# The second chunk of a first pass by seven products instead of eight, with the weights rounded in another order

## The chip, the cores and the metric

The kernel runs on one core of a Trainium2 chip. The metric is the device time of one execution in microseconds, the median of several runs. The engines of the core are TensorE (PE; its weight loads are listed as PEld), VectorE (DVE), ScalarE (ACT), GpSimd (POOL) and SyncE (SP), which issues the transfers.

## The reference

Two parts follow each other: a retention attention (8 batches, 8 heads, 576 tokens, 64 dimensions), and a two-layer block on its output with the activation h * erf(softplus(h)).

```python
scores = scale * np.matmul(q, k.transpose(0, 1, 3, 2))
Dmat = np.where(rel >= 0, gamma ** rel, 0.0)          # decay, gamma by head
attn_out = np.matmul(scores * Dmat, v)
x = attn_out.transpose(0, 2, 1, 3).reshape(B * S, H * D)   # 4608 x 512
h = x @ w_in                                          # w_in 512 x 2048
sp = np.maximum(h, 0.0) + np.log1p(np.exp(-np.abs(h)))
g = h * erf(sp)
return g @ w_out                                      # w_out 2048 x 512
```

## The kernel before

The 4608 tokens are nine chunks of 512, and d_ff is cut into four groups. The kernel walks all nine chunks for group 0, then for group 1, and so on (36 blocks). During group 0 it computes the attention as well, in stages that it deals out between the products: a stage is the transposes of q and k, the scores, or the outputs of 128 tokens.

A block has a first product set (x by w_in, `First`) and a second one (g by w_out, `Second`). Each is a 2 x 2 block product done by seven products of sums instead of eight (Winograd's form): four sums of the operands on each side, seven products of four matmuls each, accumulated in three PSUM tiles (a, e and g), some of which go on accumulating after they have been copied out. The first two chunks of group 0 are the exception: they use `plain`, the eight products, as 16 half-products of two matmuls.

The seven products of a block (`plain` and what is around it cut to what matters):

```python
PLAIN = 2

def operands_x(g, c):
    summed.add((g, c))
    t = x[g, c]
    # b11, b12, b21, b22: the quarters of x; t1, t2, t4: room for sums
    # ...
    if g == 0 or c < PLAIN:
        tt(t1, b12, b11, ALU.subtract)
        tt(t2, b22, t1, ALU.subtract)
        tt(b12, b22, b12, ALU.subtract)
    else:                                   # b12 was stored as the sum already
        tt(t2, b12, b11, ALU.add)
        tt(t1, b22, t2, ALU.subtract)
    if g == 0:
        store_x(c)                          # for the later groups
    tt(t4, b21, t2, ALU.subtract)
    x[g, c] = {A11: b11, A12: b21, S4: b22, A22: t4, S1: t1, S2: t2, S3: b12}

class First:
    def first(self):
        # ... a, e: PSUM tiles; t1: 128 x 2 x 512
        self.product(A11, self.a, True)
        nc.scalar.copy(out=self.t1[:, 0], in_=self.a)
        yield
        self.product(A12, e, True)
        tt(self.t1[:, 0], e, self.t1[:, 0], ALU.add)
        yield

    def middle(self):
        # ...
        self.product(S2, self.a, False)
        nc.scalar.copy(out=self.t1[:, 1], in_=self.a)
        yield
        self.product(S3, self.e, True)
        yield
        self.product(S1, self.a, False)
        nc.scalar.copy(out=self.t2[:, 1], in_=self.a)
        tt(self.t2[:, 1], self.e, self.t2[:, 1], ALU.add)
        yield

    def last(self):
        self.product(S4, self.a, False)
        nc.scalar.copy(out=self.t2[:, 0], in_=self.a)
        yield
        self.product(A22, self.e, False)
        tt(self.t1[:, 1], self.e, self.t1[:, 1], ALU.add)
        self.softplus()
        yield

    def plain(self):
        # four PSUM tiles; 4 x 4 half-products of two matmuls, a yield after each
        # after the last of a tile: nc.scalar.copy(out=(t2 if tok else t1)[:, f], in_=acc[n])

    def softplus(self):                     # ScalarE: 2 x 1024 columns
    def erf(self):                          # ScalarE: 2 x 1024 columns
    def multiply(self):                     # VectorE: t1 * s, t2 * s
    def sums(self):                         # VectorE: four sums of the activations
```

The weights come as raw parts and are rounded in steps; `round_weights(n)` issues n steps. Parts 1 to 4 of group 0 are w_in, parts 5 to 8 w_out. A part has five steps (ScalarE's two instructions first, then VectorE's, then GpSimd's multiplication and addition; for the first group's w_in VectorE does those too). After the last part of a matrix come four steps that are the four sums of its blocks:

```python
yield src, "wa", g, a, dc % 2, ["wa"] if g > 0 and dc == n_dc - 1 else []
# ...
sums = (["wb"] if g > 0 else ["wb", "wa"]) if (f, j) == (1, GP - 1) else []
yield src, "wb", g, B21 if f else B11, j, sums
```

The beginning is dealt out by a string (a: an attention stage, p: a half-product of the first chunk, w: the load of a part of the weights, a digit: so many steps of rounding, s: the store of x, k: matmuls that keep TensorE busy), then by a loop over the second chunk's half-products, then by the general loop:

```python
for what in "alkakakawkakakawwaa3awa2aaa5ppppaa5wwppa5ppawappwcppa5ppaaapp5s":
    # ...
most[0] = before_chunk(3)
attend(after_chunk(1))
store_x(1)
for step, _ in enumerate(firsts[1].plain()):
    if step % 2 == 0:
        attend(min(done[0] + 1, most[0]))
    round_weights(int(step > 1))
    if step == 1:
        firsts[0].softplus()
        firsts[0].erf()
    elif step == 5:
        firsts[0].multiply()
    elif step == 8:
        firsts[0].sums()
seconds[0].begin()
run(seconds[0].first(), (2, 2))       # two products, an attention stage after each
firsts[1].softplus()
most[0] = before_chunk(4)
for b, nxt in zip(blocks[2:], blocks[3:] + [None]):
    # ... the general loop: every later block by seven products
```

Of the kernel before, what the change touches and what calls it, by code (L numbers as in the profile page):

```python
# [2 lines left out]

# [1 line left out]

# [49 lines left out]
def kernel(  # L55
# [16 lines left out]
    n_dc = D_MODEL // P  # L72
    OH = D_MODEL // 2
    FH = D_FF // 2
    GP = 2
# [22 lines left out]
    def tt(out, in0, in1, op):  # L98
        nc.vector.tensor_tensor(out=out, in0=in0, in1=in1, op=op)  # L99
# [50 lines left out]
    def load(i, names="qkv"):  # L150
        if i < len(pieces):
            t = loaded.setdefault(i, {})
            for name in names:
                src = {"q": q, "k": k, "v": v}[name]
                if name == "q" and i < SQUARES:
                    t["q"] = load_rows(i, "q", q, 2)
                elif name == "q":
                    t["qs"] = load_squares(i, "q", q)
                    if i >= SQUARES_K:
                        t["ks"] = load_squares(i, "k", k)  # L160
                elif name == "v" or i < SQUARES_K or len(pieces[i]) == 1:
                    t[name] = load_rows(i, name, src, 4)
# [29 lines left out]
    def parts():  # L192

        w2 = w_in.rearrange("(e c d) (h f) -> c e d h f", c=n_dc, d=D, h=2)
        for g in range(n_g):
            for dc in range(n_dc):
                a = A11 if dc < 2 else A12
                src = [(heads[(e + dc) % 2], w2[dc, e, :, :, 2 * g * GW : 2 * (g + 1) * GW]) for e in range(2)]

                yield src, "wa", g, a, dc % 2, ["wa"] if g > 0 and dc == n_dc - 1 else []  # L200
            for f in range(2):
                for j in range(GP):
                    ft = f * FH // P + g * GP + j
                    src = [(slice(0, P), w_out[ft * P : (ft + 1) * P, :].rearrange("p (h o) -> p h o", h=2))]
                    sums = (["wb"] if g > 0 else ["wb", "wa"]) if (f, j) == (1, GP - 1) else []
                    yield src, "wb", g, B21 if f else B11, j, sums

    def sums_in(a11, s3, a12, a22, s1, s2, s4):
# [9 lines left out]
    def sums_out(b11, t3, b21, b22, t1, t2, t4):  # L218
# [7 lines left out]
        yield  # L226

    coming = parts()
    words = []
    most_g = [1]  # L230

    def load_weights():
        part = next(coming, None)
        if part is not None:
            t = wraw.tile([P, 2 * WP], UINT32, tag="wraw", name="wraw")
            for rows, src in part[0]:
                nc.sync.dma_start(out=t[rows].rearrange("p (h f) -> p h f", h=2), in_=src)
            words.append((t, *part[1:]))
# [49 lines left out]
    def round_weights(n=1):  # L288
        for _ in range(n):
            next(round_step, None)  # L290
# [149 lines left out]
    done = [0]  # L440

    def before_chunk(c):

        return stages.index((outputs, c * PC)) if c < n_ch else len(stages)

    def after_chunk(c):

        return stages.index((outputs, (c + 1) * PC - 1)) + 1

    def attend(upto):  # L450
        while done[0] < min(upto, len(stages)):
            of, i = stages[done[0]]
            of(i)
            done[0] += 1

    PLAIN = 2

    def load_x(g, c):  # L460
        x[g, c] = x_tile()
# [2 lines left out]
    def store_x(c):  # L464
        nc.sync.dma_start(out=xd[c], in_=x[0, c][:, :n_dc])
# [3 lines left out]
# [3 lines that stand above are left out]
        b11, b12, b21, b22 = (t[:, 2 * d : 2 * d + 2, h * TH : (h + 1) * TH] for d in range(2) for h in range(2))  # L472
        t1, t2, t4 = (t[:, n_dc + j, :].rearrange("p (d i) -> p d i", d=2) for j in range(3))
# [4 lines that stand above are left out]
        else:  # L478
# [3 lines that stand above are left out]
            store_x(c)  # L482
        tt(t4, b21, t2, ALU.subtract)
        x[g, c] = {A11: b11, A12: b21, S4: b22, A22: t4, S1: t1, S2: t2, S3: b12}
# [240 lines left out]
    firsts = [First(g, c) for g, c in order]  # L725
    seconds = [Second(f) for f in firsts]
# [8 lines left out]
    def keep_busy(n):  # L735
        for _ in range(n):
            nc.tensor.matmul(idle[:, :P], lhsT=ones, rhs=ones, start=True, stop=True)
# [4 lines left out]
    def run(steps, rounds=(), stages=1):  # L742

        for step, _ in enumerate(steps):
            attend(min(done[0] + stages, most[0]))
            round_weights(rounds[step] if step < len(rounds) else 0)
# [4 lines left out]

    for what in "alkakakawkakakawwaa3awa2aaa5ppppaa5wwppa5ppawappwcppa5ppaaapp5s":
        if what == "a":
            attend(done[0] + 1)
        elif what == "p":
            next(products)
        elif what == "s":
            store_x(0)  # L760
        elif what == "l":
            load(2, "kv")
        elif what == "c":
            nc.sync.dma_start(out=cst[:, CONST_FIRST:], in_=consts[:, CONST_FIRST:])
        elif what == "w":
            load_weights()
        elif what == "k":
            keep_busy(2)
        else:
            round_weights(int(what))  # L770
    most[0] = before_chunk(3)
    attend(after_chunk(1))
    store_x(1)
    for step, _ in enumerate(firsts[1].plain()):
        if step % 2 == 0:
            attend(min(done[0] + 1, most[0]))
        round_weights(int(step > 1))
        if step == 1:
            firsts[0].softplus()
            firsts[0].erf()  # L780
        elif step == 5:
            firsts[0].multiply()
        elif step == 8:
            firsts[0].sums()
    seconds[0].begin()
    run(seconds[0].first(), (2, 2))
    firsts[1].softplus()
    most[0] = before_chunk(4)
    for b, nxt in zip(blocks[2:], blocks[3:] + [None]):
        n = order.index((b.g, b.c))  # L790
# [9 lines left out]
        elif n + 2 < n_s:  # L800
            f = firsts[n + 1]
# [62 lines left out]
```

## Time and profile before

| what | value |
|---|---|
| time, median of 3 | 1027.61 us (1027.31 to 1028.06) |
| span of the profiled execution | 1024.0 us |
| transfers | 165.76 MB, mean 162 GB/s |
| instructions | 15958 |

In the profile, "L496" is line 496 of the kernel. L496 are the products of `First` by sums, L550 those of `plain`, L604 those of `Second`; L347 the scores, L365, L376 and L388 the outputs, L332 the transposes on TensorE and L326 those on VectorE. L99 is the helper `tt`, so its instructions are told apart by the tile that they write: x (with o as source: attention outputs; with x as source: sums), t, s, o, sT, wa, wb. L254 to L275 are the steps of rounding. One matmul of the source is two instructions in the profile (32-bit data), so a product of four matmuls is "x8".

The span in 40 equal slices of 25.6 us, as busy tenths, for orientation:

```profile
PE   9999999999999999999999999999999999999998
PEld 8787888888888888888888888888888888888887
DVE  3769777976976656656666666666567655555555
ACT  3354134234134444334343444444433333333332
POOL 2143112122312110010001001000100000000000
```

The change is in the second to fourth slice, where the attention, the rounding of the weights and the first chunks share the engines.

### The profile page before, as it was taken

What the parts mean: (1) busy time and instruction counts of PE and PEld (TensorE: products, weight loads), DVE (VectorE), ACT (ScalarE), POOL (GpSimd) and SP (SyncE); (2) the same over time, 40 slices, a digit from 0 to 9 for tenths busy, and PEclk for the clock granted to TensorE, in tenths of its full rate; (3) what the DMA queues carried; (4) which work ended last, traced back from release to release, by engine and by line L of the source; (5) the groups of instructions that cost most, each with busy time, mean ns of one, the idle gap of its engine ahead of it and who ended that gap; (6) DMA issues with size and microseconds to landing.
All of it is one profiled execution on the core that took longest, in us unless ns stands there. A gap on an engine that the chain in (4) does not pass through costs nothing.

```text
span 1024.0 us, 15958 instructions
## 1 busy us (share of the span) xinstructions
PE 1017.6 (99%) x6348; PEld 876.0 (86%) x6348; DVE 667.6 (65%) x1062; ACT 390.2 (38%) x481; POOL 122.6 (12%) x122
## 2 busy tenths in 40 slices
PE   9999999999999999999999999999999999999998
PEld 8787888888888888888888888888888888888887
DVE  3769777976976656656666666666567655555555
ACT  3354134234134444334343444444433333333332
POOL 2143112122312110010001001000100000000000
PEclk9999999999999999999999999999999999999999
DMA  9998989979974354544444345444433333444434
GB/s 200 203 242 175 232 203 223 255 150 253 244 195 150 106 161 145 165 160 154 164 147 158 124 147 162 165 144 144 144 124 124 124 131 127 131 136 131 126 88 119
DMA packets 146986, 165.76 MB, mean 162 GB/s; under 512 B 97376, under 2 KB 121568, under 8 KB 138848
## 3 DMA queue, kind: packets, MB, share of 16 engines
q1 hardware_dynamic: 144832, 163.57, 56.4%
q10 hardware_dynamic: 2080, 1.18, 0.5%
q8 instruction: 50, 0.82, 0.4%
q14 instruction: 24, 0.20, 0.1%
HBM read 117.52 MB, written 47.19 MB: 161 GB/s over the span
## 4 chain that ended last, share of the span: by engine, by line
PE 94%; DMA 3%; DVE 2%; SPq 1%; POOL 1%; issue 0%; ACTq 0%; DVEq 0%; POOLq 0%
PE a L604 24%; PE a L496 23%; PE g L604 12%; PE g L496 12%; PE e L496 6%; PE e L604 6%; PE o L365 3%; PE s L347 3%; PE o L388 2%; DMA raw_k<-in_k_dram 1%; PE o L376 1%; DMA raw_v<-in_v_dram 1%; PE f L668 1%; SPq L147 1%; PE p L550 1%; PE h L668 1%
## 5 line engine op out<-in xcount | busy, mean ns | idle before, releaser
L496 PE MATMUL a<-x,wa 128*128 128x256 f32 x1088 | 258.3, 380 | 0.0
L496 PEld LDWEIGHTS a<-x,wa 128*128 128x128 f32 x1088 | 205.7, 190 | 28.5
L604 PE MATMUL a<-wb,s 128*128 128x256 f32 x840 | 200.0, 381 | 0.0
L604 PEld LDWEIGHTS a<-wb,s 128*128 128x128 f32 x840 | 158.4, 190 | 22.9 <-ACT o L618 0.7
L99 DVE TENSOR_TENSOR t<-g,t 128x512 f32<-128x512 f32 x68 | 47.0, 691 | 151.9 <-ACT t L526 114.1
L496 PE MATMUL g<-x,wa 128*128 128x256 f32 x544 | 129.2, 380 | 0.0
L496 PEld LDWEIGHTS g<-x,wa 128*128 128x128 f32 x544 | 102.8, 190 | 14.4
L99 DVE TENSOR_TENSOR o<-a,o 128x512 f32<-128x512 f32 x104 | 71.4, 687 | 46.4 <-PE a L604 46.4
L521 ACT COPY t<-a 128x512 f32<-128x512 f32 x34 | 19.9, 586 | 188.3 <-PE a L496 188.3
L99 DVE TENSOR_TENSOR t<-t,s 128x1024 f32<-128x1024 f32 x72 | 88.4, 1267 | 0.0
L274 POOL TENSOR_TENSOR wraw<-wraw 128x512 f32<-128x512 f32 x28 | 29.4, 1051 | 438.1 <-DVE wraw L272 184.4
L565 ACT ACTIVATE s<-t 128x1024 f32<-128x1024 f32 x72 | 72.1, 1049 | 24.6 <-DVE t L99 24.5
L99 DVE TENSOR_TENSOR x<-x 128x512 f32<-128x512 f32 x115 | 75.8, 693 | 1.2
L532 ACT COPY t<-a 128x512 f32<-128x512 f32 x34 | 19.9, 586 | 144.4 <-PE a L496 144.4
L569 ACT ACTIVATE s<-s 128x1024 f32<-128x1024 f32 x72 | 72.1, 1049 | 0.4
L604 PE MATMUL g<-wb,s 128*128 128x256 f32 x280 | 66.7, 381 | 0.0
L604 PE MATMUL e<-wb,t 128*128 128x256 f32 x280 | 66.6, 380 | 0.0
L604 PE MATMUL a<-wb,t 128*128 128x256 f32 x280 | 66.6, 380 | 0.0
L604 PE MATMUL g<-wb,t 128*128 128x256 f32 x280 | 66.4, 380 | 0.0
L99 DVE TENSOR_TENSOR sT<-s,cst 128x512 f32<-128x512 f32 x72 | 46.2, 682 | 30.4 <-PE s L347 30.4
L496 PE MATMUL e<-x,wa 128*128 128x256 f32 x272 | 64.8, 381 | 0.0
L99 DVE TENSOR_TENSOR o<-g,o 128x512 f32<-128x512 f32 x70 | 47.9, 684 | 20.9 <-ACT o L618 18.1
(86 smaller groups left out, 1247.1 us busy)
## 6 DMA issues: line engine op xcount, KB each, us to landing
od<-o SPq DMA_DIRECT2D x54, 512.0 KB, 3.3
x<-xd SPq DMA_DIRECT2D x27, 1024.0 KB, 4.8
o<-od SPq DMA_DIRECT2D x27, 1024.0 KB, 5.4
raw_qs<-in_q_dram SPq DMA_DIRECT2D x96, 112.0 KB, 4.4
raw_ks<-in_k_dram SPq DMA_DIRECT2D x84, 112.0 KB, 4.2
xd<-x SPq DMA_DIRECT2D x9, 1024.0 KB, 5.2
raw_v<-in_v_dram SPq DMA_DIRECT2D x64, 128.0 KB, 4.5
wraw<-in_moe_w_in_dram SPq DMA_DIRECT2D x32, 256.0 KB, 5.7
```

Source lines behind the costliest of these rows:

```text
L99: nc.vector.tensor_tensor(out=out, in0=in0, in1=in1, op=op)
L274: engine.tensor_tensor(out=r_f, in0=high_f, in1=r_f, op=ALU.mult)
L347: nc.tensor.matmul(ps[e][:, p, :], lhsT=t["kT"][heads[e], p, :], rhs=t["qT"][heads[e], p, :], start=True, stop=True)
L365: nc.tensor.matmul(o[p % 2][heads[(e + p) % 2], p // 2, :], lhsT=t["v"][:, 2 * p + e, :], rhs=t["sT"][:, e, p, :], start=(p < 2), stop=(no ...
L388: nc.tensor.matmul(kv[heads[e], p, :], lhsT=t["k"][:, 2 * p + e, :], rhs=t["v"][:, 2 * p + e, :], start=False, stop=(p == NP - 1), skip_gr ...
L496: nc.tensor.matmul(acc[:, j * TH : (j + 1) * TH], lhsT=weights["wa", self.g][:, a, d, j * P : (j + 1) * P], rhs=x[self.g, self.c][a][:, d, :],
L521: nc.scalar.copy(out=self.t1[:, 1], in_=self.a)
L532: nc.scalar.copy(out=self.t2[:, 0], in_=self.a)
L565: nc.scalar.activation(self.s[:, j], t, AF.Softplus)
L569: nc.scalar.activation(self.s[:, j], self.s[:, j], AF.Erf)
L604: nc.tensor.matmul(acc[:, tp, :], lhsT=left[:, j * TH + tp * P : j * TH + (tp + 1) * P], rhs=weights["wb", self.g][:, b, j, :], start=(sta ...
L668: nc.tensor.matmul(acc, lhsT=left[:, j * TH + tp * P : j * TH + (tp + 1) * P], rhs=weights["wb", self.g][:, b, j, :], start=(b in (B11, B2 ...
```

## The change

The second chunk's first pass is done by seven products as well. For this the four sums of w_in must be there earlier (right after its last part, with four more steps in the string), the second chunk's x gets its four sums, and the loop over half-products becomes one over the seven products, with the steps of rounding dealt out anew: four of them at the fifth product, so that the last part of w_out is rounded ahead of the first chunk's sums of activations. In the later groups the second chunk's stored x now holds one sum ready made.

```diff
-                yield src, "wa", g, a, dc % 2, ["wa"] if g > 0 and dc == n_dc - 1 else []
+                yield src, "wa", g, a, dc % 2, ["wa"] if dc == n_dc - 1 else []
 ...
-                    sums = (["wb"] if g > 0 else ["wb", "wa"]) if (f, j) == (1, GP - 1) else []
+                    sums = ["wb"] if (f, j) == (1, GP - 1) else []
 ...
-    PLAIN = 2
+    PLAIN = 1
 ...
-    for what in "alkakakawkakakawwaa3awa2aaa5ppppaa5wwppa5ppawappwcppa5ppaaapp5s":
+    for what in "alkakakawkakakawwaa3awa2aaa5ppppaa5wwppa5ppawappwcpp4a5ppaaapp5s":
 ...
     attend(after_chunk(1))
-    store_x(1)
-    for step, _ in enumerate(firsts[1].plain()):
-        if step % 2 == 0:
+    attend(done[0] + 1)
+    operands_x(0, 1)
+    f = firsts[1]
+    for step, _ in enumerate(chain(f.first(), f.middle(), f.last())):
+        if step > 0:
             attend(min(done[0] + 1, most[0]))
-        round_weights(int(step > 1))
-        if step == 1:
+        round_weights((0, 2, 2, 2, 4, 2, 2)[step])
+        if step == 0:
             firsts[0].softplus()
             firsts[0].erf()
-        elif step == 5:
+        elif step == 2:
             firsts[0].multiply()
-        elif step == 8:
+        elif step == 4:
             firsts[0].sums()
     seconds[0].begin()
-    run(seconds[0].first(), (2, 2))
-    firsts[1].softplus()
+    run(seconds[0].first())
     most[0] = before_chunk(4)
```

More of the change, by code (lines that the diff above doesn't have):

```diff
@@ L2 @@
 from contextlib import ExitStack
+from itertools import chain
 import numpy as np
```

## The prediction

> **What bounds the kernel now.** I read the share of each engine first, then the chain that ended last, then the busy time by stage of the stretch that the change touches (45 to 97 us), then the timelines of that stretch.
>
> ```profile
> PE 1017.6 (99%) x6348; PEld 876.0 (86%) x6348; DVE 667.6 (65%) x1062; ACT 390.2 (38%) x481; POOL 122.6 (12%) x122
> ...
> PE 94%; DMA 3%; DVE 2%; SPq 1%; POOL 1%; issue 0%; ACTq 0%; DVEq 0%; POOLq 0%
> ```
>
> TensorE holds 94% of the chain, so over the whole kernel one product less is worth its own length, unless the stretch where it is saved has another limit. The busy time by stretch (busy us with the number of instructions for PE, weight loads, DVE, ACT, POOL, then clock, DMA share, GB/s) says where that could be:
>
> ```profile
> 45.00:60.00 15.00, 15.00 (x169) 12.34 (x168) 7.88 (x18) 6.39 (x12) 5.51 (x6) 1.00 0.77 196
> 60.00:70.00 10.00, 10.00 (x101) 7.92 (x100) 4.58 (x11) 8.56 (x10) 4.94 (x5) 1.00 1.19 269
> 70.00:82.00 12.00, 11.73 (x104) 9.66 (x101) 11.90 (x21) 3.72 (x7) 2.61 (x3) 1.00 1.00 226
> 82.00:97.00 15.00, 14.91 (x126) 12.11 (x128) 13.79 (x22) 9.41 (x11) 5.56 (x5) 1.00 0.85 190
> ```
>
> From 70 to 82 us VectorE is busy 11.90 of 12.00 us beside a full TensorE: two engines are at their limit at once. Before 70 us VectorE has room. The timelines of TensorE, VectorE, ScalarE and GpSimd (start, duration, instruction, in brackets the idle time before it and what ended it) show the details that the steps below use:
>
> ```profile
> 59.72 1.13 PE L550 MATMUL p<-x,wa 128*128 128x256 f32 x4
> ...
> 80.81 1.16 PE L347 MATMUL s<-qT,kT 64*128 64x128 f32 x16 [0.27 <-DVE qT L326]
> ...
> 82.87 1.89 PE L604 MATMUL a<-wb,t 128*128 128x256 f32 x8
> ...
> 86.85 1.61 PE L365 MATMUL o<-sT,raw_v 128*64 128x128 f32 x16
> ```
>
> ```profile
> 49.54 1.29 DVE L99 TENSOR_TENSOR sT<-s,cst 128x512 f32<-128x512 f32 x2 [3.45 <-PE s L347]
> ...
> 64.22 1.29 DVE L99 TENSOR_TENSOR sT<-s,cst 128x512 f32<-128x512 f32 x2 [1.69 <-PE s L347]
> 69.21 0.43 DVE L259 TENSOR_SCALAR wb<-wb 128x512 f32<-128x512 f32 x1 [3.69 <-ACT wb L254]
> ...
> 76.00 1.77 DVE L99 TENSOR_TENSOR s<-t 128x512 f32<-128x512 f32 x1
> ...
> 84.61 1.51 DVE L99 TENSOR_TENSOR wb<-wb 128x512 f32<-128x512 f32 x1 [1.18 <-POOL wb L275]
> ```
>
> ```profile
> 68.50 0.67 ACT L254 ACTIVATE wb<-wraw 128x512 f32<-128x512 f32 x1
> ...
> 84.79 0.58 ACT L618 COPY o<-a 128x512 f32<-128x512 f32 x1 [1.14 <-PE a L604]
> ```
>
> ```profile
> 75.81 1.41 POOL L275 TENSOR_TENSOR wb<-wb,wraw 128x512 f32<-128x512 f32 x1
> ```
>
> TensorE already waits 0.27 us for a transposed q at 80.81, and some 0.5 us at 86.85, where the 16 matmuls of an attention output take 1.61 us against 1.09 elsewhere (the second half of sT comes late). VectorE has holes of 3.45, 1.69 and 3.69 us before 70 us, and one of 1.18 us at 84.61.
>
> [...] the sum that starts at 76.00 takes 1.77 us while GpSimd's 1.41 us addition runs; its three neighbours, with GpSimd idle, take 0.68 or 0.69. The next such sum at 84.61 takes 1.51 beside a GpSimd multiplication. [...] at 69.21 VectorE's rounding step has waited 3.69 us for a ScalarE instruction (68.50) that stood behind softplus and erf, and nothing passed it. [...] So I take starts from starts: in the pure stage eight matmul instructions (one product) start 1.73 us apart.
>
> **The change part by part.**
>
> *TensorE.* The second chunk's first pass was 16 half-products of four matmul instructions, in six groups between attention stages. From 59.72 to 82.87 are 23.15 us; take off three transposes (0.44, 0.47, 0.43), three scores (1.09, 1.10, 1.09), two outputs (1.65, 1.48) and the wait of 0.27, and 15.13 us are left, 0.946 per half. That is 0.864 (half of 1.73) and about 0.19 per switch from an attention stage of smaller matmuls. Afterwards it is seven products, 7 x 1.73 = 12.11, in four groups, some 0.6 for the switches, and one switch of 0.19 that now falls to the first product of the second pass: 12.9. Gain on TensorE alone: 15.1 - 12.9 = 2.2, say 2.1 us (1.73 of it the eighth product). The attention stages between are the same ones in the same order.
>
> *VectorE.* Added: four sums of x (0.69 each) before the second product, and three additions on eviction (0.67 to 0.69) where ScalarE's copies sufficed; 2.8 + 2.0 = 4.8 us. The four sums of w_in (3.8 us from 89 to 94 us, with their contention) move to 46 us, into the hole of 3.45: free. The x sums start at 62.5; GpSimd works from 61.0 to 65.0, and by taking turns they end at about 67.3, t2 at 65.1. The second product that needs t2 arrives at 64.8: a wait of 0.3. The evicted first product costs nothing, it lies in the hole before 69.21. In the later passes the chunk loads its sums ready made and saves one sum each, off the path.
>
> *ScalarE.* One copy (0.5) goes ahead of softplus and erf, so w_out's third part is at VectorE at 69.6 instead of 69.2.
>
> *From 69.6 on VectorE never rests.* In the order in which the changed kernel issues: rounding, qT 0.63, two rounding steps, two multiplications 2.3, two x 0.67, a rounding step, the new addition 0.6, two sT 1.2, the last part's four rounding steps 1.9: together 9.0, to 78.6. Then GpSimd rounds the last part (1.04 + 1.28) exactly beside the four sums of activations (2.4), which contend: between 1.2 and 2.3 us more. Then qT 0.63: it ends at 82.8 to 83.9. TensorE, now earlier, wants that qT for a score at 81.4: it waits 1.4 to 2.5 us, against 0.27 before. Next come two sums of w_out and the addition that completes t1 (1.8): 84.6 to 85.7. Only then can the second chunk's softplus run (2.0), and it now stands in ScalarE's queue ahead of the copy that empties accumulator a after the first product of the second pass (before, that copy ran at 84.79, ahead of softplus). The copy ends at 87.2 to 88.3. TensorE has done score, B21 and a transpose (3.4) by 86.3 to 87.4 and waits 0.9 for it. From there T2, output, T3 and score (1.9 + 2.3 + 1.9 + 1.1) bring it to T1 at 94.4 to 95.5; with T1 the same content that was done at 96.34 is done at 96.3 to 97.4.
>
> *Sum.* TensorE's gain of 2.1 less waits of 0.3, 1.4 to 2.5 and 0.9, and 0.8 of old waits (0.27, 0.5) that these replace: from 0.3 us gained (2.1 - 2.6 + 0.8) to 0.8 us lost (2.1 - 3.7 + 0.8), which agrees with the 0.0 to +1.0 of the walk to 0.3. Behind 97 us the content is the same, and VectorE has the w_in sums less to do there.
>
> **The rivals.**
> *A. TensorE's saving arrives whole.* For it: 94% of the chain, and the wait of 1.18 us at 84.61 for GpSimd's rounding goes, as the last part is rounded ahead of the sums. Against it: 11.90 of 12.00. It would make 1025.5.
> *B. VectorE becomes the bound from 70 to 88 us,* as worked out: 1027.6 to 1028.6. Against it: the contention may be less than taking turns, and then part of the saving survives.
> *C. Transfers.* The DMA share is about 1.0 between 60 and 82 us, and TensorE asks for its k up to 2 us earlier. The raw_k for the transpose at 66.01 is issued at 59.89 and that at 74.80 at 64.23, with 4.5 us the usual landing time, so both are there. The store of the chunk's x moves behind the q load, which brings q forward. I expect no more than 0.5 us from it.
> *D. ScalarE alone:* the copy of the third product waits behind softplus and erf until about 70.7, while the fifth product, on the same accumulator, is due at 70.9: a near miss that could cost a few tenths.
>
> **Range and chances.** The walk gives +0.0 to +1.0, the ideal -2.1. I weigh the walk at two thirds, because the order is fixed and every duration is measured, and the remainder at somewhere between: 1027.8 us. Run to run, the three times of before span 0.75 us. The 8-in-10 range is 1025.9 to 1029.2: the low end is the saving nearly whole (1027.6 - 2.1 + 0.4), the high end the walk's worst with 0.6 for transfers and scatter. Two per cent would be 20.6 us, ten times the whole saving: faster by that 0.005, slower 0.005, within 0.99.
>
> **What would show it.** Right, if TensorE has eight matmul instructions less (6340) and its products in the stretch start 1.73 to 1.92 apart; if the wait of a score for qT near 81 us grows to 1.4 us or more; if a T2 product waits for ScalarE's copy near 87 us; if the activations' sums take over 3.5 us for four beside GpSimd; if VectorE is over 95% busy from 70 to 88 us; and if the T1 product of the second pass starts near 95 us. Wrong, if that T1 starts before 93.5 us (then rival A), or if TensorE waits on a transfer in 60 to 82 us (then C).

## The result and the profile after

| kernel | median | range | runs |
|---|---|---|---|
| before, the same days | 1027.46 us | 1026.00 to 1028.31 | 6 |
| changed | 1030.94 us | 1029.75 to 1031.66 | 6 |

The ratio is 1.0035, with a 95% interval of 1.0022 to 1.0048: 3.5 us slower, within 2%, but above the predicted range. The shares of the engines and of the chain, for the changed kernel:

```profile
PE 1018.0 (99%) x6340; PEld 876.5 (85%) x6340; DVE 675.9 (66%) x1066; ACT 390.0 (38%) x481; POOL 124.9 (12%) x122
...
PE 88%; DMA 4%; DVE 3%; SPq 2%; ACT 1%; issue 1%; POOL 0%; ACTq 0%; DVEq 0%; POOLq 0%
```

TensorE has its eight instructions less (6340 against 6348), and its share of the chain fell from 94 to 88%. The busy time by stretch (same columns as before: PE, weight loads, DVE, ACT, POOL, granted clock, DMA share, GB/s) says where:

```profile
70.00:82.00 12.00, 11.64 (x124) 9.35 (x120) 11.71 (x19) 5.74 (x10) 4.15 (x4) 1.00 0.92 205
82.00:97.00 15.00, 11.11 (x89) 9.20 (x90) 11.50 (x18) 6.32 (x8) 3.11 (x3) 0.77 0.60 133
```

From 82 to 97 us TensorE is busy 11.11 of 15.00 us where it was 14.91, and there the granted clock is 0.77 where it was 1.00. The timeline of TensorE shows both things in two lines:

```profile
79.78 1.99 PE L604 MATMUL a<-wb,t 128*128 128x256 f32 x8
85.89 2.08 PE L347 MATMUL s<-qT,kT 64*128 64x128 f32 x16 [4.12 <-DVE qT L326]
87.91 3.61 PE L604 MATMUL e<-wb,t 128*128 128x256 f32 x8
91.35 0.60 PE L332 MATMUL pt_k<-ident,raw_k 128*128 128x128 f32 x4
91.78 1.89 PE L604 MATMUL a<-wb,s 128*128 128x256 f32 x8
```

The score waits 4.12 us for a transposed q, and then the score takes 2.08 us (1.16 elsewhere) and the product behind it 3.61 (1.89 to 1.99 elsewhere): half speed. In slices of 0.2 us the granted clock is 0.50 from 84.4 to 91.2 us, and 1.00 on both sides. VectorE and GpSimd in the same time (L100 is the helper `tt` in the changed kernel, which was L99 before):

```profile
77.18 1.12 DVE L259 TENSOR_SCALAR wb<-wb 128x512 f32<-128x512 f32 x1
...
79.86 0.69 DVE L100 TENSOR_TENSOR s<-t 128x512 f32<-128x512 f32 x1
80.58 1.41 DVE L100 TENSOR_TENSOR s<-s,t 128x512 f32<-128x512 f32 x1
81.92 1.76 DVE L100 TENSOR_TENSOR s<-t,t 128x512 f32<-128x512 f32 x1
83.60 1.52 DVE L100 TENSOR_TENSOR s<-t,s 128x512 f32<-128x512 f32 x1
85.05 0.70 DVE L326 STREAM_TRANSPOSE qT<-raw_qs 128x512 f32<-128x512 f32 x1
```

```profile
76.73 1.28 POOL L275 TENSOR_TENSOR wb<-wb,wraw 128x512 f32<-128x512 f32 x1
80.09 1.35 POOL L274 TENSOR_TENSOR wraw<-wraw 128x512 f32<-128x512 f32 x1 [2.08 <-DVE wraw L272]
81.53 1.60 POOL L275 TENSOR_TENSOR wb<-wb,wraw 128x512 f32<-128x512 f32 x1
83.09 1.49 POOL L313 TENSOR_TENSOR raw_v<-raw_v,cst 128x512 f32<-128x512 f32 x1
```

The first of the four sums takes 0.69, as it does with GpSimd idle. The other three lie one by one beside three GpSimd instructions (two of the rounding, and L313, the weighing of v for the attention) and take 1.41, 1.76 and 1.52. The transpose for which TensorE waits stands right behind them.

A second pass has its products in the order B11, B21, T2, T3, T1 (two more follow later); T2 accumulates on in PSUM tile a, which ScalarE copies out behind B11. One measure serves for all that follows, *the stretch*: from the start of the last attention output of the second chunk (57.48 us before, 57.64 in the changed kernel) to the start of the output that follows T1 of the second pass (96.27 and 100.78). The same products and attention stages lie in it in every kernel here, apart from the eighth product. It is read from one trace of each kernel. It is 38.79 us before and 43.14 in the changed kernel: 4.35 longer. Behind the attention, the traces agree to 0.02 us (696.19 or 696.20 to the last block's final products). Between the two, the rest of the attention took 215.67 us in before and 216.87 in the changed kernel. This last difference is not counted as the change's, as the second trace of before will show.

### The profile page after: what moved, and what is told of

Same layout as the page of the kernel before. It is cut to its first block, busy times and chain, and to the rows that moved or that the text cites. A ratio compares the mean times of both kernels' runs of the same rounds, so it can differ in the third digit from the quotient of the medians.

```text
span 1029.7 us, 15946 instructions
## 1 busy us (share of the span) xinstructions
PE 1018.0 (99%) x6340; PEld 876.5 (85%) x6340; DVE 675.9 (66%) x1066; ACT 390.0 (38%) x481; POOL 124.9 (12%) x122
## 3 DMA queue, kind: packets, MB, share of 16 engines
q10 hardware_dynamic: 2080, 1.18, 0.5%
## 4 chain that ended last, share of the span: by engine, by line
PE 88%; DMA 4%; DVE 3%; SPq 2%; ACT 1%; issue 1%; POOL 0%; ACTq 0%; DVEq 0%; POOLq 0%
PE a L604 23%; PE a L496 22%; PE g L496 11%; PE g L604 11%; PE e L604 6%; PE e L496 5%; PE s L347 2%; PE o L365 2%; PE o L388 1%; SPq L148 1%; PE o L376 1%; DMA raw_k<-in_k_dram 1%; DMA raw_ks<-in_k_dram 1%; DVE t L100 1%; PE f L668 1%
## 5 line engine op out<-in xcount | busy, mean ns | idle before, releaser
L496 PE MATMUL a<-x,wa 128*128 128x256 f32 x1120 | 266.1, 380 | 0.3 <-ACT s L565 0.2
L496 PEld LDWEIGHTS a<-x,wa 128*128 128x128 f32 x1120 | 211.5, 190 | 29.9 <-issue 0.3
L100 DVE TENSOR_TENSOR t<-g,t 128x512 f32<-128x512 f32 x70 | 48.3, 690 | 150.2 <-ACT t L526 112.5
L496 PE MATMUL g<-x,wa 128*128 128x256 f32 x560 | 133.0, 380 | 0.0
L496 PEld LDWEIGHTS g<-x,wa 128*128 128x128 f32 x560 | 105.7, 190 | 14.7
L100 DVE TENSOR_TENSOR o<-a,o 128x512 f32<-128x512 f32 x104 | 71.5, 687 | 47.6 <-PE a L604 47.6
L100 DVE TENSOR_TENSOR t<-t,s 128x1024 f32<-128x1024 f32 x72 | 88.9, 1275 | 0.0
L100 DVE TENSOR_TENSOR x<-x 128x512 f32<-128x512 f32 x116 | 78.5, 710 | 1.2
L100 DVE TENSOR_TENSOR o<-g,o 128x512 f32<-128x512 f32 x70 | 48.0, 685 | 23.2 <-ACT o L618 20.5
L100 DVE TENSOR_TENSOR sT<-s,cst 128x512 f32<-128x512 f32 x72 | 46.1, 682 | 25.8 <-PE s L347 25.8
```

What stands on the lines that cost most here:

```text
L496: nc.tensor.matmul(acc[:, j * TH : (j + 1) * TH], lhsT=weights["wa", self.g][:, a, d, j * P : (j + 1) * P], rhs=x[self.g, self.c][a][:, d, :],
```

## The experiments

The long wait was one suspect, the clock another, and behind the wait stood three reasons that had to be told apart: the seven products (more for VectorE to do), the earlier rounding (GpSimd beside the sums), and the place of qT in the queue.

**1. Filling the wait.** Dummy matmuls of ones, into the PSUM tile that the next product overwrites, in front of the score.

```diff
             self.take(0, 0, self.a)
+            if (self.g, self.c) == (0, 0):
+                for _ in range(16):
+                    nc.tensor.matmul(e[:, 0, :P], lhsT=ones, rhs=ones, start=True, stop=True)
             yield
```

> The changed kernel with 16 dummy matmuls (128x128 of ones, into the PSUM tile that the next product overwrites) between the first product of the second pass and the score that waits for qT. They fill most of the 4.12 us wait and add no work for another engine. Theory 1 (a wait this long halves TensorE's clock for a while, and that costs of its own): the score and the product after it take 1.1 and 1.7 us again instead of 2.08 and 3.61, and the T1 product of the second pass, at 98.86 in the changed kernel, starts near 97.3: not the whole 2.6 us earlier, as the copy that frees accumulator a ends at 90.2 and then holds T2 (91.78 in the changed kernel). Time 1.5 us under the changed kernel, near 1029.4. Rival (the slow instructions only sit beside VectorE's delay and cost nothing): T1 stays at 98.9 and the time at 1030.9.

The timeline of TensorE with the filled wait:

```profile
82.31 3.73 PE L631 MATMUL e<-ones 128*128 128x128 f32 x32
86.61 1.16 PE L347 MATMUL s<-qT,kT 64*128 64x128 f32 x16 [0.56 <-DVE qT L326]
87.70 1.99 PE L604 MATMUL e<-wb,t 128*128 128x256 f32 x8
89.53 0.60 PE L332 MATMUL pt_k<-ident,raw_k 128*128 128x128 f32 x4
90.99 1.99 PE L604 MATMUL a<-wb,s 128*128 128x256 f32 x8 [0.86 <-ACT o L618]
```

The score and the product are back at full speed (1.16 and 1.99 us; in the second trace of this kernel the granted clock is 1.00 from 82 to 97 us, against 0.77), and T2 now waits 0.86 us for ScalarE's copy, as expected. The stretch is 41.75, 1.39 less. So the fall of the clock is a consequence of the idle wait, and it costs less than the 2.6 us of its slow instructions. The time did not show this (1031.43, 5 runs, range 1030.04 to 1032.28), so it was run again, beside a shorter filling (6 matmuls) and the changed kernel itself.

> The kernel with 16 dummy matmuls again, beside the changed kernel itself on the same chip: its stretch was 41.75 against 43.14, but its time (1031.43, 5 runs) did not show that. If the 1.4 us of the stretch reach the end, its median is 1.0 to 1.8 us under the changed kernel's here; if something behind the stretch takes them back, the medians are within 0.5.

> The changed kernel with 6 dummy matmuls in the long wait instead of 16: about 1.4 us of it filled, about 2.7 us left idle. Theory (only idleness of more than some 3 us in one piece, as the 3.1, 3.5 and 4.1 us seen so far, lowers the clock): after the wait the score takes 1.1 us and the product 1.7 to 1.8, as with 16; T2 again waits for the copy that ends at 90.2 to 90.9; the stretch is 41.7 to 42.0, the time is that of the kernel with 16. Rival (the clock falls with the share of idle time, not with one gap): the score or the product shows half speed, stretch 42.5 or more.

> The changed kernel again: 1030.9 within 0.5, stretch 43.1 within 0.2, a wait of 4.1 us within 0.1, half speed for the score and the product behind it. The rest of the attention behind the stretch between 215.7 and 216.9.

| kernel | stretch | median (runs) |
|---|---|---|
| 16 dummies, again | 41.75 | 1030.55 (6) |
| 6 dummies | 42.26 | 1030.66 (6) |
| changed kernel, again | 42.12 | 1031.18 (4) |

The expectation for the short filling failed. The timeline of TensorE there:

```profile
81.87 1.50 PE L631 MATMUL e<-ones 128*128 128x128 f32 x12
86.18 1.80 PE L347 MATMUL s<-qT,kT 64*128 64x128 f32 x16 [2.81 <-DVE qT L326]
87.91 2.97 PE L604 MATMUL e<-wb,t 128*128 128x256 f32 x8
```

A gap of 2.81 us is enough for slow work here: the score took 1.80 us (1.16 at whole speed), the product 2.97 (1.99), and the granted clock from 82 to 97 us was 0.89. Whether one gap counts or the share of idle time, as the rival says, these runs do not decide. The changed kernel did not repeat its own stretch either: 42.12 instead of 43.14, with a shorter wait and a faster product in the second trace.

```profile
85.98 2.08 PE L347 MATMUL s<-qT,kT 64*128 64x128 f32 x16 [3.75 <-DVE qT L326]
87.99 2.61 PE L604 MATMUL e<-wb,t 128*128 128x256 f32 x8
```

What the clock costs is therefore 0.4 to 1.4 us of the stretch, depending on the run. In the time it is not resolved: the medians lie 0.6 apart with ranges that overlap. By the same measure, differences of 1 us between the stretches of kernels whose clock falls mean little.

**2. qT ahead of the sums.** The sums one step later, behind the transpose; nothing else.

```diff
-        elif step == 4:
+        elif step == 5:
             firsts[0].sums()
```

> The changed kernel with the four sums of the first chunk's activations issued one step later, behind the transpose of q that the score waits for; everything else the same. Theory 1 (the wait is for the place of qT in VectorE's queue behind contended sums): the wait of 4.12 goes to under 0.5, and TensorE's clock stays whole there. But the addition that completes t1, softplus and the copy behind it in ScalarE's queue come no earlier (t1 near 87, copy done near 90), so T2 waits for the copy: T2 at 90.2 to 91.0, T1 near 97.5 to 98.3, time 1029.5 to 1030.3. [...] Rival (VectorE's extra work is what counts wherever it stands): the same, 1030.9, within 0.5.

The timeline of TensorE:

```profile
81.95 1.16 PE L347 MATMUL s<-qT,kT 64*128 64x128 f32 x16
83.04 1.99 PE L604 MATMUL e<-wb,t 128*128 128x256 f32 x8
88.13 0.65 PE L332 MATMUL pt_k<-ident,raw_k 128*128 128x128 f32 x4 [3.10 <-DVE x L100]
90.30 3.68 PE L604 MATMUL a<-wb,s 128*128 128x256 f32 x8 [1.52 <-ACT o L618]
```

The wait for qT is gone, and its length turns up again in two others: 3.10 us for PSUM tiles that the attention's output still holds (VectorE reads them behind the sums), and 1.52 for the copy behind softplus. The clock falls there instead, behind the second of them: the transposes behind the first wait took 0.65 us, as elsewhere (0.60 to 0.66), the product behind the second 3.68 (1.99 elsewhere), and the granted clock from 82 to 97 us was 0.89. The stretch is 43.21, the time 1032.18 (4 runs; ratio 1.0044, 1.0028 to 1.0061): no gain, where 1029.5 to 1030.3 was expected. I had foreseen the wait for the copy, not the one for the tiles. The four sums take 0.68 or 0.69 each in this trace, yet they end at 87.1: the two sums of w_out that now stand ahead of them take 1.19 and 1.52 beside GpSimd, and VectorE waits 1.18 us for GpSimd's addition between the two. So the place of qT alone is not the cause, and up to here the rival, VectorE's amount of work, fits as well; run 6 decides that.

**3. The seven products alone.** The last part rounded behind the sums again, as before the change.

```diff
-        round_weights((0, 2, 2, 2, 4, 2, 2)[step])
+        round_weights((0, 2, 2, 2, 1, 3, 4)[step])
```

> The seven products alone: the changed kernel with the last part of w_out rounded behind the sums of activations, as in the kernel before (steps 1, 3, 4 at the fifth to seventh product instead of 4, 2, 2). Theory 1 (rounding ahead puts GpSimd's two instructions beside the sums, and they contend): the sums end near 80.5 instead of 85.05, the score waits under 0.5 us, and the wait moves to the B21 product, which needs GpSimd's addition (done near 85.4, a wait of 2.6[...]). T1 near 95 to 96, time 1027.5 to 1028.5. Rival (the seven products themselves bring too much for VectorE): T1 stays over 98 and the time over 1030.

All four sums now take 0.68 or 0.69 us, and the score does not wait, as expected. The timeline of TensorE shows the waits that are left:

```profile
86.14 1.13 PE L604 MATMUL e<-wb,t 128*128 128x256 f32 x4 [1.23 <-POOL wb L275]
...
88.24 1.97 PE L604 MATMUL a<-wb,s 128*128 128x256 f32 x8 [0.53 <-DVE wb L100]
```

The stretch is 39.48, the time 1028.37 (20 runs; ratio 1.0009, 1.0002 to 1.0016). So with the old order of rounding the seven products come to within 0.7 us of the kernel before; what they save goes into waits, among them one of 1.23 us (2.6 expected) for the rounding that now comes last.

**4. The other part alone.** The kernel before with its eight products, the last part rounded ahead of the sums.

```diff
-        round_weights(int(step > 1))
+        round_weights((0, 0, 1, 1, 1, 1, 2, 2, 2, 0, 1, 1, 1, 1, 0, 0)[step])
```

> The other part alone: the kernel before, with its eight products, but the last part of w_out rounded ahead of the first chunk's sums of activations. Measured from the start of the last attention output of the second chunk (57.48 us before) to the output that follows T1 of the second pass (96.27), the stretch is 38.79 us before, 43.14 in the changed kernel and 39.48 with the seven products alone. Theory (rounding ahead puts GpSimd's two instructions beside the sums, with qT behind them): the sums take about 5 us, qT ends near 83.3, the score that waited 0.27 us waits 2.5 to 3, the stretch is 41 to 41.6, the time 1029.5 to 1030. Rival (rounding ahead hurts only because TensorE comes earlier with seven products): the score waits under 1 us, the stretch is 38.5 to 39.3, the time 1027.3.

The timeline of TensorE:

```profile
84.74 1.16 PE L347 MATMUL s<-qT,kT 64*128 64x128 f32 x16 [3.48 <-DVE qT L326]
85.83 1.59 PE L550 MATMUL pg<-x,wa 128*128 128x256 f32 x4
87.22 3.16 PE L604 MATMUL a<-wb,t 128*128 128x256 f32 x8
```

The four sums take 0.68, 1.41, 1.77 and 1.53 us, as in the changed kernel. The score that waited 0.27 us waits 3.48, the clock falls (0.89 from 82 to 97 us, against 1.00 before), the stretch is 43.44, the time 1033.09 (4 runs; ratio 1.0055, 1.0040 to 1.0070), all more than expected. The earlier rounding alone costs at least as much as the whole change: with it in place, seven products for eight win 0.3 us of the stretch (43.44 to 43.14), or 1.3 by the changed kernel's second trace.

**5. GpSimd's two instructions left out.** For the last part of w_out in the first group only, so that this part keeps fewer bits and the kernel's output is less exact; all else runs.

```diff
-            engine.tensor_tensor(out=r_f, in0=high_f, in1=r_f, op=ALU.mult)
-            engine.tensor_tensor(out=a_f, in0=a_f, in1=r_f, op=ALU.add)
+            if (name, g, slot, j) != ("wb", 0, B21, GP - 1):
+                engine.tensor_tensor(out=r_f, in0=high_f, in1=r_f, op=ALU.mult)
+                engine.tensor_tensor(out=a_f, in0=a_f, in1=r_f, op=ALU.add)
```

> The changed kernel without GpSimd's multiplication and addition for the last part of w_out of the first group (leaves out the low bits of that part of the weights; all else runs). Theory 1 (contention with these two makes the four sums of activations take 5.2 us instead of 2.4): the sums take 2.4 to 3.5, qT comes at 82 to 83, the score waits 0.5 to 1.5 us, the clock stays whole, T2 waits under 1 us for the copy, T1 near 95, time 1027 to 1028. Rival (the extra sums and additions are the matter, not the contention): the score still waits 3 us or more, T1 over 97.5.

The sums take 0.68 or 0.69 each, the clock stays whole (1.16 us for the score, 1.99 for the product behind it), and T2 waits 0.86 for the copy, as expected. The stretch is 39.81. But qT ended at 84.79 (82 to 83 expected), and the score waits longer. The timelines of TensorE, VectorE and GpSimd show why (line numbers behind the edit are higher by one here):

```profile
84.94 1.16 PE L348 MATMUL s<-qT,kT 64*128 64x128 f32 x16 [1.83 <-DVE qT L327]
```

```profile
78.15 1.12 DVE L259 TENSOR_SCALAR wb<-wb 128x512 f32<-128x512 f32 x1
79.31 1.15 DVE L263 TENSOR_SCALAR wb<-wb 128x512 uint32<-128x512 uint32 x1
```

```profile
77.70 1.29 POOL L276 TENSOR_TENSOR wb<-wb,wraw 128x512 f32<-128x512 f32 x1
78.95 1.23 POOL L314 TENSOR_TENSOR raw_v<-raw_v,cst 128x512 f32<-128x512 f32 x1
```

Both rounding steps take 0.43 alone. The first lies beside the addition for the third part, as it does in the changed kernel (1.12 there too). The second is new: GpSimd went on to its next instruction, the weighing of v, and that now lies beside it. So 0.7 us of the contention moved there, but 3.33 us of the stretch went with the two instructions (43.14 to 39.81). The time is 1029.38 (20 runs; ratio 1.0017, 1.0010 to 1.0024); that is above the 1027 to 1028 I expected, though well under the changed kernel.

**6. The same work in another order.** Rounding ahead as in the change, but behind it first qT, the addition that completes t1 and the attention's output (these two read PSUM), then two sums of w_out, and only then the sums of activations. The other two sums of w_out follow behind the first products of the second pass, which do not need them.

```diff
-            assert ("wb", self.g) in rounded
+            assert ("wb", self.g) in rounded or b in (B11, B21)
 ...
-        round_weights((0, 2, 2, 2, 4, 2, 2)[step])
+        round_weights((0, 2, 2, 2, 4, 0, 2)[step])
 ...
-        elif step == 4:
+        elif step == 6:
             firsts[0].sums()
 ...
-    run(seconds[0].first())
+    run(seconds[0].first(), (1, 1))
```

> The changed kernel in another order: the last part rounded ahead as in it, but then qT, the addition that completes t1 and the attention's output first, which read PSUM and lie beside GpSimd's rounding, then two sums of w_out, and only then the four sums of activations (the last two sums of w_out behind the first products of the second pass). Theory (not VectorE's amount of work but which of it lies beside GpSimd and ahead of qT sets the wait): no wait for qT, t1 complete near 81, the copy free of softplus by 84, T2 waits under 1 us, clock whole, stretch 37.0 to 38.3 against 38.79 before, time 1025.9 to 1027.2. Rival (VectorE's amount of work sets it): a wait of 2 us or more turns up at T2 or at the output behind it, stretch 39.5 or more, time 1028 or more.

VectorE's timeline, from where GpSimd rounds the last part (81.33 to 83.75 in this trace):

```profile
81.10 0.70 DVE L326 STREAM_TRANSPOSE qT<-raw_qs 128x512 f32<-128x512 f32 x1
81.73 0.65 DVE L100 TENSOR_TENSOR t<-g,t 128x512 f32<-128x512 f32 x1
82.30 0.41 DVE L100 TENSOR_TENSOR x<-o,cst 128x256 f32<-128x256 f32 x1
82.63 0.41 DVE L427 TENSOR_TENSOR state<-o,cst 128x256 f32<-128x256 f32 x1
82.96 0.41 DVE L100 TENSOR_TENSOR x<-o,cst 128x256 f32<-128x256 f32 x1
83.29 2.46 DVE L100 TENSOR_TENSOR wb<-wb 128x512 f32<-128x512 f32 x2
85.67 0.68 DVE L100 TENSOR_TENSOR s<-t 128x512 f32<-128x512 f32 x1
```

Beside GpSimd the transpose (0.70) and the four instructions that read PSUM (0.65 and 0.41) keep their lengths. Only the two sums of w_out meet the end of the rounding and the weighing of v (2.46 for two, against 1.28 elsewhere). No score waits; T2 waits 0.41:

```profile
83.30 1.16 PE L347 MATMUL s<-qT,kT 64*128 64x128 f32 x16
...
87.22 1.97 PE L604 MATMUL a<-wb,s 128*128 128x256 f32 x8 [0.41 <-DVE s L100]
```

The stretch is 37.82, the time 1027.20 (12 runs; ratio 1.0000, 0.9991 to 1.0008), both as expected. VectorE has as many instructions as in the changed kernel (1066 in the whole execution), so their amount is not what made it wait; the order is. How much each of the moves brings by itself was not measured.

**7. And the third part earlier.** As 6, with a part of the rounding moved to where VectorE had waited 1.15 us for ScalarE (70.12 us in the changed kernel).

```diff
-        round_weights((0, 2, 2, 2, 4, 0, 2)[step])
+        round_weights((1, 3, 0, 2, 4, 0, 2)[step])
```

> The reordered kernel with the third part of w_out started one product earlier as well, so that three of its steps on VectorE fall before 70 us, where VectorE waited 1.15 us for ScalarE. Theory: VectorE is 0.5 to 1 us ahead from 70 us on, which takes what is left of the waits: stretch 0.3 to 0.8 under the reordered kernel's. Against it: softplus of the first chunk comes 1.2 us later and the copy of the third product behind it, so the fifth product can wait up to 1 us: stretch the same or 0.5 more.

The busy time by stretch, TensorE first and VectorE third:

```profile
70.00:82.00 12.00, 11.88 (x132) 9.92 (x132) 11.86 (x21) 7.64 (x12) 4.70 (x5) 1.00 1.06 237
82.00:97.00 15.00, 15.00 (x164) 11.91 (x164) 11.59 (x20) 6.15 (x8) 3.03 (x3) 1.00 0.82 177
```

TensorE is at 15.00 of 15.00 from 82 to 97 us. The stretch is 36.73, 1.09 under the one of 6 (0.3 to 0.8 expected), and the time is 1025.93 (20 runs, 1024.02 to 1027.70; ratio 0.9987, 0.9980 to 0.9993). It is the one kernel here that beats the kernel before, by 1.35 us between the medians. Its stretch is 2.06 us shorter than before's.

**8. The kernel before, once more,** for the scatter of its trace.

> The kernel before once more, for the scatter of its trace: the stretch should be 38.8 within 0.2. The rest of the attention behind it took 215.67 us in the first trace of before and 216.87 in that of the changed kernel; if it is over 216.3 here, that difference is scatter of the transfers and nothing of the change.

The stretch is 38.79 again, to the hundredth. The rest of the attention took 216.55 us where the first trace had 215.67. The kernels with the change had from 215.67 to 218.05 there, and the longest was the changed kernel's second trace, so a small part of its own there is not excluded. Most of the scatter between runs that have the same stretch lies there, where in the first trace of the changed kernel two scores wait 0.35 and 0.70 us for a transposed k (ahead of the first of them VectorE had waited 1.30 us for the transfer of that k), and before 57 us, where TensorE waits for transfers of q and k (0.29 and 0.39 us in the first trace of before).

## Why the prediction was wrong

*TensorE's saving* was right: 2.1 us predicted. Up to the second pass it was 25.39 - 22.14 = 3.25 us from the start of the stretch, less the score that moved behind (1.09) and 0.09 of waits, so 2.07.

*The free places* were right: the sums of w_in went into the hole at 46 us (the next sT at 49.80 against 49.54), the x sums ended at 67.1 (67.3 walked), and the product that needs t2 waited 0.18 (0.3 walked).

*The failed step* is the one on VectorE from 69.6 us: "which contend: between 1.2 and 2.3 us more", qT at "82.8 to 83.9" and a wait of "1.4 to 2.5 us". qT ended at 85.75 and the wait was 4.12. The mechanism and its place were right: VectorE the bound, qT behind sums that lie beside GpSimd. Three terms were too small. VectorE's run began 0.5 later (70.12). A rounding step beside GpSimd's addition took 1.12 instead of 0.43, where I had counted contention for sums of two inputs alone, which the trace of before shows (1.77 and 1.51 against 0.69). And the sums took 5.19 us (79.86 to 85.05) instead of 3.6 to 4.7: I had left out GpSimd's third instruction, the weighing of v, which followed at 83.09.

*What was left out altogether* is the clock. I took every duration from an unbroken TensorE, but a wait as long as this one (4.12 us) makes the work behind it slow: the granted clock fell to 0.50, and the score and the product took 2.08 and 3.61 us instead of 1.16 and 1.99. A gap of 2.81 us sufficed for slow work as well. Filled, the wait costs 0.4 to 1.4 us less of the stretch.

*The wait of T2* for the copy, walked as 0.9, is not in the changed kernel: the copy ended at 90.2 (87.2 to 88.3 walked), but TensorE came even later, at 91.78. It appears as soon as the clock is whole (0.86 and 0.87 with the dummies).

*The sum.* The walk gave 0.0 to +1.0 and weighed it at two thirds; the rest of the weight lay on the side of a gain. The stretch says +3.3 to +4.35, the time +3.5. The seven products alone bring 0.69 us, and the earlier rounding on top of them 3.66 of the 4.35 (2.64 of 3.33 by the second trace). The two do not simply add: the earlier rounding alone brings 4.65. Of the rivals, A's first ground was real (the wait of 1.18 for GpSimd is gone) and worth nothing there; the earlier rounding saved that wait and paid for it with the sums. B held, larger. C and D were small: no transfer held TensorE between 60 and 82 us.

*What I missed in weighing* is that the order was not a fixed fact but the thing to ask about. Runs 6 and 7 do the same work as the changed kernel in another order, and with the second of them the stretch is 2.06 us shorter than before's, about TensorE's own saving of 2.07.

## What to carry to other kernels

Before an instruction is moved ahead on one engine, list what it will then lie beside on the other engines, and look up in a trace how long each of these instructions takes there. Here, beside GpSimd, three sums with two SBUF inputs took 1.41 to 1.76 us instead of 0.69 and single-input rounding steps 1.11 to 1.15 instead of 0.43, while a transpose (0.70) and instructions that read PSUM (0.65 and 0.41) kept their lengths; so the latter were put there. Where two engines are full at once, walk the queue of the second up to each instruction that the first waits for, and put that one ahead of work that has a later deadline. A wait of TensorE like the one of 2.81 us here is to be priced with the slow work behind it (1.80 us for a score of 1.16, 2.97 for a product of 1.99).

## What was not expected of the hardware

Gaps of TensorE and the speed behind them: behind 1.83 us (run 5) the score and the product took 1.16 and 1.99 us, whole speed. Behind 2.81 (6 dummies), 3.48 (run 4) and 3.75 us (the changed kernel again) the granted clock fell, to a mean of 0.89 from 82 to 97 us, and behind 4.12 us (the changed kernel) to a mean of 0.77; with 3.10 and 1.52 us and one transpose group between them (run 2) the mean was 0.89. The fall does not come at a fixed point of the wait. In slices of 0.2 us, the granted clock of the changed kernel went to 0.50 some 2.6 us after the wait began (84.4), so the score behind it took 2.08 us. With 6 dummies the score took 1.80. In run 4 it still took 1.16, and only the half-product and the product behind it were slow (1.59 and 3.16 against 1.03 to 1.13 and 1.89 to 1.99 elsewhere). In the changed kernel the clock then stayed at 0.50 for 6.8 us. If it was 0.50 in the other four as well, a mean of 0.89 is some 3.3 us of it, an estimate; that is about half. The product behind the score took 3.61 us in the first trace of the changed kernel and 2.61 in the other, with 0.77 and 0.89. And VectorE's single-input rounding steps (128x512, 32 bits) took 1.11 to 1.15 us beside an instruction of GpSimd, against 0.43.
